# A Fourier transform, a mixture of experts and a gated network in one kernel: a row store moved behind the first gathers, fold tails on VectorE, routing steps placed later

## The chip, the core and the metric

The kernel runs on one core of one Trainium2 chip. The metric is the time of one execution on the device in microseconds. The core's engines work side by side, each through its own list of instructions in order, and wait for one another by semaphores: TensorE (matrix products, with its own queue of weight loads), VectorE (DVE in the profile), ScalarE (ACT), GpSimd (POOL) and SyncE (SP), which here only issues transfers. Sixteen DMA engines carry the transfers that SyncE and GpSimd issue.

## What is computed

The reference transforms the input, sends each row to one of eight experts, and puts the result through a second network:

```python
X = np.fft.fft(np.fft.fft(x, axis=1), axis=2).real        # x: (8, 3072, 256)
x = X.reshape(24576, 256)
logits = x @ w_gate                                       # 8 experts
expert_idx = np.argmax(logits, axis=1); probs = softmax(logits)
# each expert takes the first 768 rows that chose it, in order; other rows give 0
h = np.maximum(np.einsum('ecd,edf->ecf', disp, w1), 0.0)  # (8, 768, 1024)
y = np.einsum('ecf,efd->ecd', h, w2)                      # (8, 768, 256)
out[i] = gate_w[i] * y[expert_idx[i], pos[i]]             # kept rows
h = out @ w_in                                            # (24576, 2048)
return (h / (1 + np.exp(-1.702 * h))) @ w_out
```

At most 6,144 of the 24,576 rows are kept, and since every expert takes the first that choose it, they come from the first rows. The kernel therefore transforms only two and a half of the eight batches, and has a second path behind a condition for inputs where that is not enough.

## The kernel before

A batch (3072 x 256) is a pair of half batches, "units" of 1536 rows; units 0 to 4 are made. For each batch there are two stages on TensorE. In the **S stage** (`fft_s`) the transform along the sequence is a product with cosine and sine tables. A batch's input comes in three parts j, each 1 MB, loaded by SyncE into one of three buffers. Part j is first folded (`fft_fold`): five additions and subtractions on VectorE and a tail of five small instructions (two copies of one column, an addition, a subtraction, a memset), on VectorE for the very first part of the kernel and on GpSimd for all others (line 465). ScalarE then makes `fhi`, a rounded copy, and VectorE the rest `flo`; for j = 2 two small transfers move halves of the part in between. TensorE multiplies in three passes, `fhi` with the table's high and low part (`chi`, `clo`) and `flo` with the high one, and sums into tiles in its accumulation memory, one of eight banks each: `psP0`, `psP2`, `psPE`, `psPO` and the same for Q. The parts are taken in the order 0, 1, 2 in the first batch and 0, 2, 1 in the others. `fft_s_end` combines the tiles on ScalarE and VectorE to `hiP` and `hiQ`. The **row stage** (`fft_d`) multiplies these with the table of the second axis, twelve row tiles t, each a tile `pd` of 128 rows for either half batch, and ScalarE copies them to `xtok`; the logits come out with them.

**Routing** of a unit (`choose`, `count`, `route`) finds each row's expert, its place among the expert's rows and its weight: a chain of some 25 small instructions on VectorE with the counting products `pp` of `oh` on TensorE in the middle. It ends with a store of the unit's rows from `xtok` to the buffer `rows` in device memory, 1.56 MB (or half of it), issued by GpSimd, and with `hold`, which queues the unit for `hold_tables` (tables `lt` and `ls`; VectorE makes both, GpSimd multiplies `lt`) and `hold_sum` (the product `pl`, which turns them into a list of row numbers per expert, `held`). `slots` makes the index list `heldi` from it, and with that GpSimd's indirect transfers gather the rows of a block, three tiles of 128 rows.

The **expert part** takes blocks of 384 rows, 16 in all: `ffn1` for the expert's two layers, `ffn2` for the second network. The first three blocks are those of experts 0 to 2 from units 0 to 2; their gathers are issued in the last row stage, while unit 3's rows and unit 4's are still being routed and stored. For a block VectorE scales the gathered tiles (`xr`, line 878), TensorE transposes them (`pt`, line 898), ScalarE and VectorE split the result to `xhi` and `xlo`. Weights come in pieces of 256 KB, which ScalarE and VectorE split to a high and a low part (`w1h`, `w1l`, `w2h`, `w2l`; lines 355 and 356). SyncE also writes zeros to the output (`zero_out`), 96 stores of 256 KB, two at every second step f of the blocks 0 to 6, the rest later.

The order of an engine's instructions is made by a scheduler from the order in the program, the dependencies and the free buffers and banks; `after` adds an edge that holds for the order alone. So a routing step's place in the program (the hooks `counts` in the S stage and `mid` in the row stage) sets its place on every engine. `CHOOSE` and `ROUTE` are the row tiles of batch 1 at which the first half of unit 2 is chosen and routed. Unit 0 is routed in the middle of batch 1's first part, unit 1 right behind that part, the two halves of unit 2 at row tile 10 of batch 1 and in the first part of batch 2, unit 3 at row tile 2 of batch 2, unit 4 in the first block.

Of the kernel before, what the change touches and what calls it, by code (L numbers as in the profile page):

```python
# [32 lines left out]
ROW = 260  # L33
# [13 lines left out]
LAG = 6  # L47
D1 = 3

J0, J1 = (0, 1, 2), (0, 2, 1)  # L50
# [1 line left out]

FOLD = ((0, "s", 6), (0, 8, 11))
SPLIT = (1,)
CHOOSE, ROUTE = 6, 10
EARLY = 11
LATE, HELD = 3, 7
IN0, IN1 = 5, 7
# [113 lines left out]
class K:  # L172
# [15 lines left out]
    def setup(self):  # L188
        nc, tc = self.nc, self.tc
        enter = self.ctx.enter_context  # L190
        self.c0 = c0 = enter(tc.tile_pool(name="c0", bufs=1))
        self.xr = enter(tc.tile_pool(name="xr", bufs=XR))
        self.ps = enter(tc.tile_pool(name="ps", bufs=8, space=PSUM))
        self.dram = enter(tc.tile_pool(name="dr", bufs=1, space=DRAM))
        n = P + 5 * HT * E // 2 + 3 * HT
        self.smt = c0.tile([P, n], F32, name="smt")
        self.tri = c0.tile([P, 5, P], F16, name="tri")
        self.ident = self.smt[:, 0:P]
        o = P
        self.wt = self.smt[:, o : o + HT * E].rearrange("p (t e) -> p t e", e=E)  # L200
        o += HT * E
        self.seg = {HT: self.smt[:, o : o + HT * E], HT // 2: self.smt[:, o + HT * E : o + 3 * HT * E // 2]}
        self.place = self.smt[:, n - 3 * HT : n - 2 * HT]
        self.tok = self.smt[:, n - 2 * HT : n].rearrange("p (h t) -> p h t", h=2)
        self.base = c0.tile([P, E], F32, name="base")
        self.flag = c0.tile([P, 1], F32, name="flag")
        nc.vector.memset(self.flag, 1.0)
        self.nop = c0.tile([1, 1], F32, name="nop")
        self.sig = c0.tile([1, 1], F32, name="sig")
        nc.vector.memset(self.sig, 0.0)  # L210
        self.disp = self.dram.tile([self.nslot, ROW], F32, name="disp")

        self.rows = self.dram.tile([1 + self.nu * S // 2, ROW], F32, name="rows")
        nst = E * self.capt
        self.held = c0.tile([P, nst], F32, name="held")
        self.heldi = [c0.tile([P, nst], I32, name=f"heldi{i}") for i in range(2)]
        self.idx = None
        self.todo, self.made = [], []
        zt = c0.tile([P, ROW], F32, name="zt")
        nc.gpsimd.memset(zt, 0.0)  # L220
        nc.gpsimd.memset(zt.bitcast(I32)[:, 257:258], OOB)
        self.zt = zt
        nc.gpsimd.dma_start(out=self.rows[0:1, :], in_=zt[0:1])
# [286 lines left out]
    def fft_s(self, b, j, data, hook=lambda i: None):  # L510
        nc = self.nc
        dh, dl = data
        pt, cnt = self.pt, self.cnt
        last = j == JS(b)[-1]
        work = [(half, c, terms) for half in "PQ" for c, terms in self.terms(half, j)]
        if last and j != 2:
            work.sort(key=lambda v: v[1] in (0, 2))
        elif last:
            work.sort(key=lambda v: v[0] == "Q" and v[1] in (0, 2))
        for i, (half, c, terms) in enumerate(work):  # L520
            hook(i)
            n = KC if c == 0 else KC - 2
            at_ = (half, c)
            if at_ not in pt:
                pt[at_] = self.ps.tile([P, KC], F32, name=f"ps{half}{c}", tag="ps")
                cnt[at_] = 0
            row = half == "Q" and c in (0, 2)
            tot = 3 * NJ + row
            ops = [(u[:, g, i, :], w[j][:, t, :n]) for (g, i), t in terms
                   for (u, w) in ((dh, self.chi), (dh, self.clo), (dl, self.chi))]  # L530
            if row and last:
                ops.append((self.sel, self.trs[:, c // 2, :n]))
            for lhsT, rhs in ops:
                nc.tensor.matmul(pt[at_][:, :n], lhsT=lhsT, rhs=rhs, start=(cnt[at_] == 0),
                                 stop=(cnt[at_] == tot - 1))
                cnt[at_] += 1
# [93 lines left out]
    def route(self, xt, mir, u=None, t0=0, chosen=None):  # L630
# [4 lines left out]
        nc = self.nc  # L635
        V = nc.vector
        rp = self.rp
        n = xt.shape[1]
# [34 lines left out]
        V.tensor_copy(out=xt[:, :, 257:258].bitcast(I32)[:, :, 0], in_=tok)  # L673
        if u is not None:
            v = self.rows[1 + u * HT * P : 1 + (u + 1) * HT * P].rearrange("(p i) w -> p i w", i=HT)
            nc.gpsimd.dma_start(out=v[:, t0 : t0 + n], in_=xt[:, :, 0:ROW])
            self.hold(u, t0, n, sloti, pos)
        if u is None or u < self.nu // 2 * 2:
            V.tensor_scalar(out=tok, in0=tok, scalar1=float(S), scalar2=None, op0=ALU.add)
# [319 lines left out]
def kernel(ctx, tc, cap, x, xed, xeb, xt, cm, dc, dct, tri, sel, sm, wg, w1, w2, wi, wo, out):  # L999
# [32 lines left out]
    def fold(b, j):  # L1032
        if b < nb:
            while (b, j) not in xq:
                xload()
            data[j] = k.fft_fold(xq.pop((b, j)), j, (b, j) == (0, J0[0]))

    loads = iter([(b, j) for b in range(1, nb) for j in J1])

# [15 lines left out]
    def route_next():  # L1055
        b, mir, xt, t0, chosen = units.pop(0)
        u = 2 * b + mir
        k.route(xt, mir, u, t0, chosen)
        if u == ua and t0 + xt.shape[1] == HT:
            k.check_full(min(na, cap))  # L1060
# [6 lines left out]
    for b in range(nb):  # L1067
        k.fft_s_begin(b)
        for i, j in enumerate(JS(b)):
            if b == 0 and i == 2:  # L1070
                k.fft_dtables()

            def counts(n, i=i):
                if (i, n) == (0, 4) and units:
                    route_next()
                if b == 0 and (i, n) == (2, 5):
                    k.fft_rows()
                if (b, i, n) == (2, 1, 3):
                    k.hold_tables(2)

            k.fft_s(b, j, data.pop(j), counts)
            while i == 0 and units and b == 1:
                route_next()
            if (b, i) == (1, 0):
                k.hold_tables(2)
            if i == 0 and b:
                folds(b - 1, "n")
        if b == 0:
# [15 lines left out]
        def mid(t):  # L1104
            if b == 1 and t == 0:
                k.hold_sum(2)
                k.hold_tables(2)
            if b == 1 and t == 9:
                k.hold_sum(2)
            if b == 2 and t == 0:  # L1110
                with tc.high_priority():
                    k.hold_sum(2)
                    k.slots(ua)
                xrs[0] = k.ffn_gather(*work[0])
            if b == 2 and t == 2:
                route_next()
                k.hold_tables(2, k.last_gather)
                for n in range(1, AHEAD):
                    xrs[n] = k.ffn_gather(*work[n])
            if t == EARLY and b + 1 == nb and xrs:  # L1120
                xins[0] = k.ffn_in(xrs[0], work[0][2], k.los[2])
            folds(b, t)
            if b in SPLIT and t == CHOOSE:
                xt = xs[0][:, : HT // 2]
                units.append((b, 0, xt, 0, k.choose(xt)))
            if b in SPLIT and t == ROUTE:
                route_next()

        xs = [next(k.slot) for _ in range(1 + (2 * b + 1 < nu))]
        k.fft_d(PQ, xs, mid)  # L1130
# [69 lines left out]
    for n, (e, i0, ns) in enumerate(work):  # L1200
        last = n + 1 == len(work)

        def hook(f, n=n, last=last):
# [22 lines left out]
            if n:  # L1226
                for _ in range(PACE[f]):
                    w64step()
            if f % 2 == 0 and n <= LAG:
                zstep(ZC // 3)  # L1230

        def hook2(f, n=n):
# [96 lines left out]
```

## Time and profile before

| | before |
|---|---|
| three timed runs, median (lowest to highest) | 985.06 us (983.24 to 985.53) |
| the profiled execution, its span | 980.04 us, 978.4 us |
| TensorE, VectorE, ScalarE, GpSimd busy | 925.4, 609.1, 509.7, 225.9 us |
| granted clock of TensorE, mean | 0.98 |
| TensorE idle ahead of its first product | 13.2 us |
| HBM read, written | 51.02, 39.47 MB |

The span runs from the first to the last instruction that the profiler saw. "Busy" adds up an engine's instructions. A list of waits says which engine's instruction ended an idle time. The granted clock is the share of full speed, 2.4 GHz, that TensorE was given; 0.50 is its other level, 1.2 GHz.

### The profile page before, as it was taken

The page shows a single profiled execution, that of the slowest core. Times are in us where ns is not written, and L with a number is a line of the kernel's source. Part 1 is how long each engine was busy: PE and PEld are TensorE (multiplying, and loading weights), DVE is VectorE, ACT ScalarE, POOL GpSimd, SP SyncE. Part 2 cuts the span into 40 slices and gives each one's busy share as a digit, 9 for nine tenths or more (in the row PEclk, how much of TensorE's full clock was granted, in tenths as well). Part 3 has the DMA queues.
Part 4 walks back from the last instruction along what each step waited for, and adds up shares of the span by engine and source line. Part 5 has one row for each costly group of instructions (what it writes and reads, how often), then busy time and mean ns, then how long its engine had stood idle before and what let it go on. Part 6 is the DMA issues. An engine that isn't in the chain of part 4 may idle for free. (4 is left out here: it accounts for less than half of the span.)

```text
span 978.4 us, 15881 instructions
## 1 busy us (share of the span) xinstructions
PE 925.4 (95%) x5950; PEld 904.2 (92%) x5950; DVE 609.1 (62%) x1178; ACT 509.7 (52%) x1056; POOL 225.9 (23%) x259
## 2 busy tenths in 40 slices
PE   3898979999899999999999999999999999999995
PEld 3686769999789999999999999999999999999995
DVE  6688789988994556454645464756535555555552
ACT  4555546656654555354644464646444554555452
POOL 6534525667751011111111100001010110011011
PEclk9899979999899999999999999999999999999998
DMA  8263898978810026001700030301000000000000
GB/s 321 96 189 120 231 290 267 318 246 274 263 45 17 17 87 206 17 18 46 246 17 18 12 92 2 102 1 60 1 17 1 17 17 1 18 17 17 1 17 20
DMA packets 65614, 92.03 MB, mean 94 GB/s; under 512 B 5886, under 2 KB 54262, under 8 KB 64374
## 3 DMA queue, kind: packets, MB, share of 16 engines
q1 hardware_dynamic: 58870, 70.23, 21.9%
q0 software_dynamic: 6656, 20.68, 7.0%
q8 instruction: 49, 0.80, 0.3%
q14 instruction: 39, 0.32, 0.1%
HBM read 51.02 MB, written 39.47 MB: 92 GB/s over the span
## 5 line engine op out<-in xcount | busy, mean ns | idle before, releaser
L975 DVE TENSOR_TENSOR sg<-ph,sg 128x384 f32<-128x384 f32 x256 | 142.7, 557 | 118.0 <-ACT sg L974 117.6
L979 DVE TENSOR_TENSOR gl<-sg,gh 128x384 fp32r<-128x384 f32 x256 | 147.3, 575 | 108.1 <-ACT gh L978 105.7
L978 ACT CAST gh<-sg 128x384 fp32r<-128x384 f32 x256 | 131.1, 512 | 121.1 <-DVE sg L975 121.1
L974 ACT ACTIVATE sg<-ph 128x384 f32<-128x384 f32 x256 | 125.8, 492 | 110.1 <-PE ph L970 105.8
L992 POOL DMA_INDIRECT out<-orow,ix x48 | 47.6, 992 | 558.3 <-ACT orow L991 548.5
L931 DVE SCALAR_TENSOR_TENSOR hl<-ph,hh 128x384 fp32r<-128x384 f32 x128 | 70.9, 554 | 78.8 <-ACT hh L930 78.4
L930 ACT ACTIVATE hh<-ph 128x384 fp32r<-128x384 f32 x128 | 62.8, 493 | 78.9 <-PE ph L925 78.1
L925 PE MATMUL ph<-xhi,w1h 128*128 128x384 f32 x256 | 87.0, 340 | 0.4 <-ACT xhi L355 0.4
L916 PE MATMUL py<-hh,w2h 128*128 128x384 f32 x256 | 87.0, 340 | 0.0
L925 PE MATMUL ph<-xhi,w1l 128*128 128x384 f32 x256 | 86.7, 339 | 0.0
L916 PE MATMUL py<-hl,w2h 128*128 128x384 f32 x256 | 86.0, 336 | 0.6 <-DVE hl L931 0.6
L925 PE MATMUL ph<-xlo,w1h 128*128 128x384 f32 x256 | 86.5, 339 | 0.0
L916 PE MATMUL py<-hh,w2l 128*128 128x384 f32 x256 | 85.6, 334 | 0.0
L864 POOL DMA_INDIRECT xr<-rows,heldi x48 | 52.4, 1092 | 71.2 <-PE pt L898 54.2
L925 PEld LDWEIGHTS ph<-xhi,w1h 128*128 128x128 f32 x256 | 48.9, 191 | 0.8 <-ACT xhi L355 0.8
L916 PEld LDWEIGHTS py<-hl,w2h 128*128 128x128 f32 x256 | 48.0, 188 | 1.3 <-DVE hl L931 1.2
L925 PEld LDWEIGHTS ph<-xlo,w1h 128*128 128x128 f32 x256 | 48.9, 191 | 0.3
L925 PEld LDWEIGHTS ph<-xhi,w1l 128*128 128x128 f32 x256 | 48.9, 191 | 0.0
L916 PEld LDWEIGHTS py<-hh,w2l 128*128 128x128 f32 x256 | 48.1, 188 | 0.0
L916 PEld LDWEIGHTS py<-hh,w2h 128*128 128x128 f32 x256 | 48.1, 188 | 0.0
L356 DVE TENSOR_TENSOR w2l<-wraw,w2h 128x512 fp32r<-128x512 f32 x44 | 36.5, 835 | 16.2 <-ACT w2h L355 15.5
L355 ACT CAST w2h<-wraw 128x512 fp32r<-128x512 f32 x44 | 27.5, 624 | 10.5 <-PE py L916 9.5
(365 smaller groups left out, 2736.3 us busy)
## 6 DMA issues: line engine op xcount, KB each, us to landing
out<-zt SPq DMA_DIRECT2D x96, 256.0 KB, 4.5
wraw<-in_w SPq DMA_DIRECT2D x88, 256.0 KB, 3.4
x<-in_x SPq DMA_DIRECT2D x9, 1024.0 KB, 6.2
rows<-xtok POOLq DMA_DIRECT2D x3, 1560.0 KB, 10.2
wraw<-in_wi SPq DMA_DIRECT2D x8, 512.0 KB, 5.3
wraw<-in_wo SPq DMA_DIRECT2D x8, 512.0 KB, 4.1
cr<-in_cm SPq DMA_DIRECT2D x6, 388.0 KB, 8.2
rows<-xtok POOLq DMA_DIRECT2D x2, 780.0 KB, 7.0
```

What stands on the lines that cost most here:

```text
L355: h = nc.scalar.copy(out=hi, in_=src)
L356: return h, nc.vector.tensor_tensor(out=lo, in0=src, in1=hi.bitcast(F32), op=ALU.subtract)
L864: self.last_gather = nc.gpsimd.indirect_dma_start(out=xr[:, i, :], out_offset=None, in_=self.rows[0 : self.nrow], in_offset=bass.IndirectO ...
L916: nc.tensor.matmul(py[a][:, :n], lhsT=w2[f // 2][v][:, f % 2, a * P : (a + 1) * P], rhs=(hh, hl)[u][:, :n], start=(f == 0 and k == 0), sto ...
L925: nc.tensor.matmul(ph[:, :n], lhsT=w1[f // 2][v][:, a, (f % 2) * P : (f % 2 + 1) * P], rhs=(xh, xl)[u][:, a, :n], start=(k == 0), stop=(k ...
L930: self.last_a = nc.scalar.activation(out=hh[:, :n], in_=ph[:, :n], func=AF.Relu)
L931: self.last_v = nc.vector.scalar_tensor_tensor(out=hl[:, :n], in0=ph[:, :n], scalar=0.0, in1=hh[:, :n].bitcast(F32), op0=ALU.max, op1=ALU. ...
L974: nc.scalar.activation(out=sg[:, :n], in_=ph[:, :n], func=AF.Sigmoid, scale=1.702)
L975: nc.vector.tensor_tensor(out=sg[:, :n], in0=ph[:, :n], in1=sg[:, :n], op=ALU.mult)
L978: nc.scalar.copy(out=gh[:, :n], in_=sg[:, :n])
L979: nc.vector.tensor_tensor(out=gl[:, :n], in0=sg[:, :n], in1=gh[:, :n].bitcast(F32), op=ALU.subtract)
L992: ins = nc.gpsimd.indirect_dma_start(out=out, out_offset=bass.IndirectOffsetOnAxis(ap=xr[:, i : i + 1], axis=0), in_=orow, in_offset=None, ...
```

## The change

It has four parts. The tail of the fold runs on VectorE for all three parts of batch 0, not for the first alone. In `route` the store of a unit's rows is ordered behind the last gather issued so far; there is one when unit 3 is routed, the third tile of block 0. The routing steps stand elsewhere: unit 0 behind the first part of batch 1's S stage, unit 1 three tiles into its second part, the two halves of unit 2 in the first part of batch 2 and behind it; `ROUTE` goes. The second part of these S stages takes its O tiles last, so that two `pp` can have a bank each. And the first block issues no zero stores; the eight follow later.

```diff
-CHOOSE, ROUTE = 6, 10
+CHOOSE = 6
...
+        self.last_gather = None
...
             work.sort(key=lambda v: v[0] == "Q" and v[1] in (0, 2))
+        elif j == 2:
+            work.sort(key=lambda v: v[1] == "O")
...
-            nc.gpsimd.dma_start(out=v[:, t0 : t0 + n], in_=xt[:, :, 0:ROW])
+            ins = nc.gpsimd.dma_start(out=v[:, t0 : t0 + n], in_=xt[:, :, 0:ROW])
+            self.after(ins, self.last_gather)
...
-            data[j] = k.fft_fold(xq.pop((b, j)), j, (b, j) == (0, J0[0]))
+            data[j] = k.fft_fold(xq.pop((b, j)), j, b == 0)
...
             def counts(n, i=i):
-                if (i, n) == (0, 4) and units:
+                if (b and (i, n) == (1, 0)) or (b, i, n) == (2, 0, 3):
                     route_next()
+                if (b, i, n) == (1, 1, 2):
+                    route_next()
+                    k.hold_tables(2)
                 if b == 0 and (i, n) == (2, 5):
                     k.fft_rows()
-                if (b, i, n) == (2, 1, 3):
+                if (b, i, n) == (2, 1, 4):
                     k.hold_tables(2)
 
             k.fft_s(b, j, data.pop(j), counts)
-            while i == 0 and units and b == 1:
-                route_next()
-            if (b, i) == (1, 0):
-                k.hold_tables(2)
...
-            if b in SPLIT and t == ROUTE:
-                route_next()
...
-            if f % 2 == 0 and n <= LAG:
+            if f % 2 == 0 and 0 < n <= LAG:
                 zstep(ZC // 3)
```

Line numbers of the changed program are 1 to 4 higher. The first place is VectorE in the first half batch; `x` are the parts being folded. Before, between the two `flo` of parts 0 and 1 (the last rows of it):

```order
L462 TENSOR_TENSOR x<-x 128x512
L463 TENSOR_TENSOR x<-x 128x512
L457 TENSOR_TENSOR x<-x 128x512
L458 TENSOR_TENSOR x<-x 128x512
L462 TENSOR_TENSOR x<-x 128x512
L463 TENSOR_TENSOR x<-x 128x512
L356 TENSOR_TENSOR flo<-x,fhi 128x1024
```

After, the same stretch from the second row on:

```order
L464 TENSOR_TENSOR x<-x 128x512
L458 TENSOR_TENSOR x<-x 128x512
L468 COPY x<-x 128x1
L469 COPY x<-x 128x1
L470 TENSOR_TENSOR x<-x 128x256
L471 TENSOR_TENSOR x<-x 128x256
L459 TENSOR_TENSOR x<-x 128x512
L472 MEMSET x 128x2
L463 TENSOR_TENSOR x<-x 128x512
L464 TENSOR_TENSOR x<-x 128x512
```

The tail of part 1 stands among the folds of part 2, and the tail of part 2 (the same five rows) follows this and comes ahead of `flo` of part 1.

The second place is VectorE at the end of batch 1's S stage. Before, the four last instructions that make `hiP` and `hiQ`, and what follows them:

```order
L551 TENSOR_TENSOR hiQ<-eb,psQO 128x384
L557 SCALAR_TENSOR_TENSOR hiQ<-psQO,ngs,t_720 128x384
L458 TENSOR_TENSOR x<-x 128x512
L455 TENSOR_TENSOR x<-x 128x1024
L462 TENSOR_TENSOR x<-x 128x512
L463 TENSOR_TENSOR x<-x 128x512
L731 TENSOR_TENSOR held<-held,pl 128x48
```

After, first a piece further ahead in unit 0's routing, then `hiQ`:

```order
L617 TENSOR_TENSOR oh<-eq,q 128x12x8
L459 TENSOR_TENSOR x<-x 128x512
L657 TENSOR_TENSOR pp<-pp,base 128x8
L652 TENSOR_SCALAR q<-q 128x12
L463 TENSOR_TENSOR x<-x 128x512
L357 TENSOR_TENSOR flo<-x,fhi 128x1024
L658 SCALAR_TENSOR_TENSOR inc<-smt,pp 128x96
L464 TENSOR_TENSOR x<-x 128x512
L659 TENSOR_TENSOR sel<-pp,inc 128x8x12
L671 COPY base<-inc 128x8
L456 TENSOR_TENSOR x<-x 128x1024
```

```order
L554 TENSOR_TENSOR hiQ<-eb,psQO 128x384
L698 SCALAR_TENSOR_TENSOR sf<-ti,pos 128x12
L699 CAST tf<-ti 128x12
L560 SCALAR_TENSOR_TENSOR hiQ<-psQO,ngs,t_720 128x384
L735 TENSOR_TENSOR held<-held,pl 128x48
```

The four folds of batch 2's parts that stood behind `hiQ` stand ahead of it among the routing, and one more (line 458) follows between these two pieces.

The third place is GpSimd's queue and VectorE in the last row stage. GpSimd before, from unit 2's second store on (`xr` are the gathers, `xtokx` is unit 3's buffer):

```order
L676 DMA rows_75<-xtok_92 128x6x260
L711 TENSOR_TENSOR lt_1015<-lt_1015,smt_66 128x288
L711 TENSOR_TENSOR lt_1020<-lt_1020,smt_66 128x288
L676 DMA rows_75<-xtokx_93 1536x1x260
L864 DMA xr_1172<-rows_75,heldi0_77 128x260 x3
L864 DMA xr_1246<-rows_75,heldi0_77 128x260 x3
L864 DMA xr_1256<-rows_75,heldi0_77 128x260 x3
```

After:

```order
L679 DMA rows_75<-xtok_92 128x6x260 x2
L715 TENSOR_TENSOR lt_1018<-lt_1018,smt_66 128x288
L715 TENSOR_TENSOR lt_1023<-lt_1023,smt_66 128x288
L868 DMA xr_1172<-rows_75,heldi0_77 128x260 x3
L679 DMA rows_75<-xtokx_93 1536x1x260
L868 DMA xr_1246<-rows_75,heldi0_77 128x260 x3
L868 DMA xr_1256<-rows_75,heldi0_77 128x260 x2
```

VectorE before, from the second gathered tile's scaling on, twelve rows ahead of the third tile's:

```order
L878 TENSOR_SCALAR xr<-xr 128x256
L693 TENSOR_SCALAR ti<-sloti 128x12
L694 SCALAR_TENSOR_TENSOR sf<-ti,pos 128x12
L695 CAST tf<-ti 128x12
L356 TENSOR_TENSOR w1l<-wraw,w1h 128x512
L356 TENSOR_TENSOR w2l<-wraw,w2h 128x512
L710 TENSOR_TENSOR lt<-tf,tri 128x288
L356 TENSOR_TENSOR w1l<-wraw,w1h 128x512
L356 TENSOR_TENSOR w2l<-wraw,w2h 128x512
L713 TENSOR_TENSOR ls<-sf,tri 128x768
L710 TENSOR_TENSOR lt<-tf,tri 128x288
L713 TENSOR_TENSOR ls<-sf,tri 128x768
```

After, from the second tile's scaling on:

```order
L882 TENSOR_SCALAR xr<-xr 128x256
L662 TENSOR_TENSOR sel<-sel,oh 128x96
L669 TENSOR_TENSOR base<-inc,pp 128x8
L663 TENSOR_REDUCE pos<-sel 128x12
L882 TENSOR_SCALAR xr<-xr 128x256
L665 TENSOR_TENSOR over<-pos,q 128x12
L887 TENSOR_SCALAR ix<-xr 128x3
L667 SCALAR_TENSOR_TENSOR sloti<-over,pos 128x12
L697 TENSOR_SCALAR ti<-sloti 128x12
L357 TENSOR_TENSOR w1l<-wraw,w1h 128x512
L357 TENSOR_TENSOR w2l<-wraw,w2h 128x512
```

Unit 3's store went behind the third gather, and the third tile's scaling from behind the four weight splits to ahead of them; the two `lt` and two `ls` still come ahead of `xlo`.

## Rows read from the trace of the kernel before

**Rows 1.** TensorE's waits over the whole span: total us, times, longest us.

```profile
PE psP L534 <- ACT fhi L355: 19.5, 3, 13.2
PE pp L623 <- DVE oh L614: 2.4, 1, 2.4
PE pp L623 <- DVE ex L647: 2.1, 1, 2.1
PE pp L623 <- DVE smt L679: 1.1, 1, 1.1
```

**Rows 2.** Stretches: busy us and instructions by engine, granted clock, DMA share, GB/s.

```profile
core 0: us, PE busy (x) PEld busy (x) DVE busy (x) ACT busy (x) POOL busy (x), PEclk, DMA share, GB/s
23.50:29.40 5.90, 5.49 (x16) 4.98 (x17) 5.70 (x6) 5.00 (x9) 5.90 (x10) 0.50 0.04 14
29.70:31.10 1.40, 1.40 (x9) 1.15 (x7) 0.00 (x0) 0.66 (x2) 1.32 (x7) 1.00 0.00 0
75.32:91.17 15.85, 13.46 (x80) 9.99 (x79) 13.05 (x27) 9.81 (x28) 8.30 (x12) 1.00 0.28 80
91.17:108.06 16.89, 15.81 (x78) 14.57 (x76) 16.86 (x68) 7.36 (x14) 4.96 (x9) 0.90 0.65 189
128.60:135.40 6.80, 6.35 (x20) 5.95 (x21) 4.50 (x18) 2.53 (x6) 1.05 (x1) 0.50 0.71 254
400.00:978.00 578.00, 567.05 (x3867) 566.63 (x3865) 304.17 (x569) 288.42 (x601) 50.76 (x51) 0.99 0.10 33
```

**Rows 3.** Time order, 10 to 36 us: start us, us, engine, line, operation, idle before.

```profile
10.98 0.15 DVE L467 COPY x<-x 128x1 f32<-128x1 f32 x1
...
12.03 1.05 ACT L355 CAST fhi<-x 128x1024 fp32r<-128x1024 f32 x1 [2.51 <-DVE x L471]
...
18.42 1.19 POOL L467 COPY x<-x 128x1 f32<-128x1 f32 x1 [4.02 <-DVE x L463]
...
22.48 1.04 ACT L355 CAST fhi<-x 128x1024 fp32r<-128x1024 f32 x1 [3.92 <-POOL x L471]
...
23.43 1.58 ACT L315 ACTIVATE chi<-cr 128x772 fp32r<-128x772 f16 x2
...
23.57 0.69 PE L534 MATMUL psP<-chi,fhi 128*128 128x386 f32 x1 [3.12 <-ACT fhi L355]
...
27.40 1.11 ACT L315 ACTIVATE clo<-cr,alt 128x384 fp32r<-128x384 f16 x2
...
33.27 1.04 ACT L355 CAST fhi<-x 128x1024 fp32r<-128x1024 f32 x1 [2.01 <-DMA x<-x]
...
34.36 0.44 PE L534 MATMUL psP<-chi,fhi 128*128 128x386 f32 x1 [3.20 <-ACT fhi L355]
```

**Rows 4.** Time order, VectorE from 58 to 76 us.

```profile
58.49 1.23 DVE L455 TENSOR_TENSOR x<-x 128x1024 f32<-128x1024 f32 x1 [3.69 <-DMA x<-in_x]
...
70.02 0.63 DVE L662 TENSOR_TENSOR over<-pos,q 128x12 f32<-128x12 f32 x1
...
74.65 0.90 DVE L557 SCALAR_TENSOR_TENSOR hiQ<-psQO,ngs,t 128x384 f32<-128x384 f32 x1
...
75.99 1.21 DVE L455 TENSOR_TENSOR x<-x 128x1024 f32<-128x1024 f32 x1
```

**Rows 5.** Time order, 108 to 132 us; last the gathers' us from issue to landing.

```profile
108.98 0.99 POOL L676 DMA_DIRECT2D rows<-xtokx  x1 [3.19 <-DVE xtokx L672]
110.34 1.14 POOL L864 DMA_INDIRECT xr<-rows,heldi  x1 [0.38 <-DVE heldi L737]
...
124.52 0.62 ACT L355 CAST w2h<-wraw 128x512 fp32r<-128x512 f32 x1 [0.78 <-DMA wraw<-in_w]
...
127.89 0.76 DVE L878 TENSOR_SCALAR xr<-xr 128x256 f32<-128x256 f32 x1
...
128.70 0.69 PE L898 MATMUL pt<-smt,xr 128*128 128x128 f32 x2 [7.78 <-DVE xr L878]
...
131.19 0.52 PE L925 MATMUL ph<-xlo,w1h 128*128 128x384 f32 x1
...
DMA to landing us min/median/max: 4.4/6.4/8.6
```

## What the change should do, worked out

> **What bounds the kernel now.** TensorE is busy for 95% of the span. The list of what it waited for, read first, shows where the rest is: at `fhi` in the transform, at the counting products `pp`, and at one transpose [rows 1, 5], all ahead of 137 us. In the long second part it has hardly a gap and the DMA engines are a tenth busy [rows 2], so a microsecond gained ahead of it comes out of the total, unless a later wait takes it back. I therefore went gap by gap through the time order of each engine from 0 to 137 us [rows 3 to 5], with the granted clock of the stretches beside it [rows 2]. The times are those of the profiled run, 980.04 us in all (span 978.4). The three timed runs have a median of 985.06, 5.0 above it; I form the sum on the profiled run and carry it over to the median.
>
> A gap costs more than its length. From 23.5 to 29.4 and from 128.6 to 135.4 us, after TensorE had been idle for 3.12 and 7.78 us, the granted clock is 0.50, the 1.2 GHz level, and products start 0.32 us apart; from 29.7 to 31.1, at 2.4 GHz, 0.17 to 0.18 us apart [rows 2]. Such a stretch loses half of its busy time.
>
> **1. The first half batch (0 to 44 us).** TensorE waits 3.12 us at 23.57 and 3.20 us at 34.36, both for ScalarE's `fhi` [rows 3]. The first `fhi` stands behind GpSimd's tail of the fold, from 18.42 to just ahead of 22.48 us, the second behind the same tail and a copy by DMA. The change puts these two tails, five instructions each, on VectorE. What that costs there is seen at the first fold, which has always done it: from the tail's first copy at 10.98 to ScalarE's start at 12.03 it is 1.05 us. VectorE ends the fold just ahead of 18.42, does one fold instruction of 0.6 us, then the tail: it ends at about 19.9, and `fhi` starts 2.6 us earlier than at 22.48. TensorE (busy until 20.45) goes on at 21.1, does four products and then needs `flo`, which now stands behind the second tail: two fold instructions (1.2 us), the tail (1.0) and `flo` (1.5) end at about 23.9. Twenty products more at 0.18 us end at 27.5. ScalarE meanwhile has eight conversions of the third table, from 23.43 to 28.5 in the old run, now right behind the first `fhi`: 20.9 to 26.0 us; two copies of 0.4 us and the third `fhi` follow, and TensorE starts on it at 27.9, not 34.36: 6.5 us earlier. If the clock falls again as it did, the twenty products take 6.4 us, end at 30.3, and the gain is 4.0. I take **-6.0 us** (-6.5 to -4.0), near the first end, because the gap is shorter. The loads that follow are issued when a fold gives its buffer back, so they move along; GpSimd's prelude, which stood behind the tails, only comes earlier.
>
> **2. Routing later, O tiles last (57 to 110 us).** Three gaps at `pp` end here, 2.1, 2.4 and 1.1 us [rows 1]; with the slow stretch behind the two long ones (1.6 us each, half of 3.4) that is 8.8 us. In the new order `pp` stands nine products later in the second batch (1.6 us), and for the split half batch a whole stage later. But the next to be late is VectorE. From 58.49, where it waited 3.69 us for a load of x, it has hardly a pause until `hiQ` ends at 75.55, and TensorE's row stage starts on that at 75.3 to 75.8 [rows 4]. The new order puts five fold instructions ahead of `hiQ` that stood behind it: one like that at 75.99 (1.1 us) and four of half its width (0.6 each), 3.5 us; some 0.7 us of waiting for `pp` comes off. So `hiQ` ends near 78.4. TensorE, done at about 73, stands for 5 us and does the start of its row stage at the lower clock: 2.8 us for `hiQ` and 2 to 3 for the clock. The stage (15.85 us from 75.32) loses its 2.4 us gap, so it ends 2.5 us later than 91.17. The third batch, 16.9 us of which 15.8 are busy and some 3 of these slow [rows 2], has neither gap nor slow stretch and takes 14.2: TensorE is level again. VectorE, which carries the 2.5 us on and saves about 1 of it, ends the third batch's `hiQ` 1 to 1.5 us later, and the first gather starts 1 us later, counted without part 1. I take **+1.0 us**. Bounds: -4, if VectorE keeps up and the gaps just go; +4, if it loses as much again to GpSimd as the 0.63 us at 70.02 for 12 elements shows (0.15 for a copy as small at 10.98) [rows 3, 4].
>
> Here the Trainium skill has a rule: "SBUF — State Buffer", section "SBUF: two separate sides", says that VectorE with two inputs from SBUF and a GpSimd instruction take one shared port pair as an exclusive lock, and the later one stands still. The row at 70.02, which ran beside a GpSimd product, agrees in kind; by this rule the new order, with GpSimd's products in a row, would lose more there, as in rival C.
>
> **3. The first gathers (108 to 137 us).** TensorE waits 7.78 us at 128.70 for the scaling of the third gathered tile, which VectorE does at 127.89 [rows 5]. That is not the gather alone: this scaling stands behind four weight splits, and these behind ScalarE's conversion at 124.52, which waited for its load. These loads were in flight with the store of the fourth half batch, 1.56 MB, issued at 108.98, 1.4 us ahead of the first gather. Gathers take 4.4 us to land at best and 8.6 at worst [rows 5]. The change issues the store behind three gathers, takes the zero stores out of this stretch, and the order that results scales the third tile ahead of the four splits. Count from the first gather, 110.34 in the old run. The third is issued 2.8 us later and lands 6 us after that (between 4.4 and 8.6; the store is gone at first, 1 MB of weights is not): 8.8. Then VectorE scales (0.7 with its neighbours), does four splits (0.6 each), two `lt` and two `ls` (2.5 together) and the first `xlo` (0.5): 14.9. The products that can run without `xlo` are done by then. In the old run the first product with `xlo` starts at 131.19, 20.85 behind the first gather. That is 5.9 us; TensorE now stands twice for 2 to 3 us instead of once for 7.8, and of the 2 us that the lower clock cost after 131.19 I credit 0.6. **-6.5 us**; -10 if the gathers land in 4.4 us and the clock stays up, -2.5 if the weights land as late as before and hold up the splits.
>
> Here the skill has a rule that speaks against the change: "DMA: Bandwidth & Descriptors", section "Queues, rings and completion order", says that a DMA engine takes the queues that have work in turn, packet by packet, so that a store which is issued later still takes its share from the weights. By it the total is that of rival B. No row here separates the two; gathers beside the store took up to 8.6 us.
>
> **4. Zero stores.** Eight stores of 256 KB leave the first block and follow in the seventh block and on, where the DMA engines are a tenth busy [rows 2]. TensorE had no wait for a weight in the first block either. **0 us** (-0.5 to +0.5). The store that goes behind the gathers is read by gathers of the fourth block, some 30 us on; that covers it.
>
> **Sum.** -6.0 + 1.0 - 6.5 + 0 = -11.5 us: 968.5 for the profiled run, **973.5 us** for the median. All good ends together give -21 (964), all bad ones -2 (983).
>
> **Rivals.**
> A, VectorE is not late at the row stages: part 2 brings -4 and the total -16.5, 968.5 us. For it: VectorE stood 3.7 us ahead of this stretch. Against: that wait is for a load that moves along.
> B, the entry still waits for weights: the gathers are there, the splits are not. Part 3 brings -2.5, the total -7.5, 977.5 us. For it: the conversion at 124.52 waited for its load. It is also the case in which the store's place doesn't do what the change says.
> C, slower: VectorE, held up by GpSimd's products, ends the second batch's `hiQ` so late that TensorE stands there and starts its row stage at 1.2 GHz. The slow stretch costs up to 3.4 us (6.8 at half speed, the longest in [rows 2]), every microsecond of `hiQ` counts in full, and the gaps that go give back 5. To eat the 12.5 us of parts 1 and 3, `hiQ` must end some 14 us later than 75.55; at 17 us the total is 988. Against: the 17 us from 58.49 to 75.55 would have to take nearly twice their time.
> D, no difference: the bad ends of all parts at once, 982 to 984 us.
>
> **How the numbers follow.** Forecast 0.55, A 0.20, B 0.13, C 0.05, D 0.07. A measurement of this kernel can tell about 0.3%, 3 us, from no change. Faster by more than that are the forecast, A and B: 0.88; within it D: 0.07; slower C: 0.05. The range 965 to 981 leaves out C, D and the far end of A, somewhat under 2 in 10.
>
> **What would show it.** Right: TensorE's waits for the second and third `fhi` are together under 2.5 us; none is left at `pp`; there is a new wait ahead of the second batch's row stage, at a `pe` or `pd`, with a slow stretch behind it; the first three gathers land in 7 us or less, and the wait at the transposes is under 3 us. Wrong in part 1: over 5 us for the third `fhi`. Wrong in part 2: `hiQ` at its old place, or over 5 us late. Wrong in part 3: the first product with `xlo` more than 18 us behind the first gather.

## The result and the profile after

| | before | after |
|---|---|---|
| side by side, median (lowest to highest) | 984.15 us (978.50 to 985.53), 4 runs | 970.86 us (969.38 to 972.65), 4 runs |
| ratio, 95% interval | | 0.9876 [0.9834, 0.9919] |
| after once more, with more runs of before beside it | 980.63 us, 17 runs | 970.37 us, 6 runs |
| ratio, 95% interval | | 0.9894 [0.9864, 0.9924] |
| the profiled execution, its span | 980.04 us, 978.4 us | 972.65 us, 971.0 us |
| TensorE, VectorE, ScalarE, GpSimd busy | 925.4, 609.1, 509.7, 225.9 us | 923.0, 610.0, 509.1, 227.4 us |

The kernel is 10 to 13 us faster: 973.5 us were predicted, 970.9 measured. The profiled pair differs by only 7.4 us, since the profiled execution of before, 980.04 us, lies below three of the four timed beside it, and that of after is the slowest of its four. Two single executions in the experiments below, of 1833 us (u_route) and 1520 us (o_route), are slow runs and stand in no median. The total came out as predicted; its terms did not, as the traces show below. What TensorE waited for after the change, over the whole span (total us, times, longest us), to be read beside [rows 1]:

```profile
PE psP L537 <- ACT fhi L356: 15.5, 2, 13.3
PE ph L929 <- ACT xhi L356: 3.6, 1, 3.6
PE pt L902 <- DVE xr L882: 2.8, 3, 1.8
PE psP L537 <- DVE flo L357: 2.1, 1, 2.1
PE pd L574 <- DVE ti L697: 1.5, 1, 1.5
PE pp L626 <- DVE pp L657: 0.7, 1, 0.7
```

The wait for the third `fhi`, the long ones at `pp` and the 7.8 us at the first block's transposes are gone. New are 2.1 us for `flo`, 1.5 at the first `pd`, 3.6 for ScalarE's `xhi`, and 1.8 at the transposes of the second block.

**The first half batch.** Time order (start us, us, engine, line, operation, idle before), to be read beside [rows 3]:

```profile
19.12 0.14 DVE L468 COPY x<-x 128x1 f32<-128x1 f32 x1
20.66 1.04 ACT L356 CAST fhi<-x 128x1024 fp32r<-128x1024 f32 x1 [1.98 <-DVE x L472]
21.76 0.44 PE L537 MATMUL psP<-chi,fhi 128*128 128x386 f32 x1 [2.16 <-ACT fhi L356]
22.10 0.86 DVE L470 TENSOR_TENSOR x<-x 128x256 f32<-128x256 f32 x1
23.53 1.22 DVE L357 TENSOR_TENSOR flo<-x,fhi 128x1024 fp32r<-128x1024 f32 x1
24.80 1.01 PE L537 MATMUL psP<-chi,flo 128*128 128x386 f32 x2 [2.07 <-DVE flo L357]
27.43 1.05 ACT L356 CAST fhi<-x 128x1024 fp32r<-128x1024 f32 x1
31.20 0.34 PE L537 MATMUL psP<-chi,fhi 128*128 128x386 f32 x1
```

The third `fhi` is ready at 28.5 us, 0.6 later than worked out, but TensorE comes to it only at 31.20: it stood twice for 2.1 us, and then the clock was low. The third part starts 3.2 us earlier than at 34.36, not 6.5.

That is one execution. In another of the same program (a_again below) TensorE stood for 2.07 and 2.06 us in the same two places, and the clock came back sooner (two products, then the stretch from 24 to 31 us, to be read beside the one below):

```profile
24.63 1.01 PE L537 MATMUL psP<-chi,flo 128*128 128x386 f32 x2 [2.06 <-DVE flo L357]
29.58 0.34 PE L537 MATMUL psP<-chi,fhi 128*128 128x386 f32 x1
...
24.00:31.00 7.00, 6.37 (x29) 6.37 (x30) 5.64 (x8) 4.60 (x10) 6.77 (x12) 0.76 0.71 201
```

In the eight traces that have part 1 as in the change (after, a_again, u_store, u_zero, u_route, i_late, i_xr, and i_flo, where one copy has moved) the third part starts between 29.58 and 31.42 us and the product `pw` at the end of the half batch between 32.36 and 34.19; in the four without it (before, u_fold, o_store, o_route) it is 34.30 to 34.43 and 37.25 to 38.63.

**The stages behind it.** Stretches (busy us and instructions by engine, granted clock, DMA share, GB/s), to be read beside [rows 2]: the slow stretch in the first half batch, the row stage of batch 1, the S stage of batch 2, and a stretch at the start of the second block.

```profile
24.00:31.00 7.00, 6.20 (x19) 6.20 (x20) 5.80 (x8) 4.77 (x10) 6.77 (x12) 0.51 0.58 176
72.62:84.99 12.37, 12.23 (x72) 9.58 (x73) 12.37 (x23) 8.04 (x24) 6.13 (x8) 1.00 0.24 85
84.99:100.87 15.88, 14.45 (x80) 13.02 (x79) 14.99 (x69) 9.22 (x19) 6.70 (x11) 1.00 0.63 199
136.53:140.00 3.47, 3.47 (x23) 3.21 (x24) 2.67 (x7) 0.04 (x1) 0.00 (x0) 0.54 1.04 287
```

Batch 1's row stage and batch 2's S stage now run at the full clock; batch 2's S stage takes 15.88 us instead of 16.89, and ends at 100.87 instead of 108.06.

**The entry.** Time order of GpSimd's first gather and unit 3's store, ScalarE's last weight conversion ahead of the first block, and TensorE's entries to the first and second block; to be read beside [rows 5]:

```profile
103.68 1.14 POOL L868 DMA_INDIRECT xr<-rows,heldi  x1 [3.58 <-DVE heldi L741]
108.02 1.09 POOL L679 DMA_DIRECT2D rows<-xtokx  x1
115.98 0.62 ACT L356 CAST w2h<-wraw 128x512 fp32r<-128x512 f32 x1 [3.49 <-DMA wraw<-in_w]
117.33 0.88 ACT L356 CAST xhi<-pt 128x384 fp32r<-128x384 f32 x2
117.88 0.69 PE L929 MATMUL ph<-xhi,w1h 128*128 128x384 f32 x1 [3.64 <-ACT xhi L356]
135.72 1.28 DVE L882 TENSOR_SCALAR xr<-xr 128x256 f32<-128x256 f32 x3
136.53 1.64 PE L902 MATMUL pt<-smt,xr 128*128 128x128 f32 x6 [1.80 <-DVE xr L882]
```

TensorE now stands because ScalarE, whose queue has `xhi` behind the last `w2h`, waits 3.49 us for that weight to land. And at the second block it stands again, for a scaling that VectorE does behind unit 4's tables, and runs the 3.5 us behind that at a granted clock of 0.54.

How far the run is ahead of the profiled run of before, at points in the order of time:

| point | before | after | ahead by |
|---|---|---|---|
| first product `pw`, end of the first half batch | 37.25 | 33.97 | 3.28 |
| first `psP` of batch 2 | 91.17 | 84.99 | 6.18 |
| first `pd` of batch 2 | 108.06 | 100.87 | 7.19 |
| first gather | 110.34 | 103.68 | 6.66 |
| first product with `xlo` | 131.19 | 120.11 | 11.08 |
| transposes of the second block | 146.45 | 136.53 | 9.92 |
| transposes of the fourth block | 183.28 | 175.53 | 7.75 |

From there to the last block the lead stays at 7.8 to 7.9 us. So in this pair part 1 gave 3.3 us, part 2 gave 3.4 at the gather, the entry 4.4, and the second and third block took 3.3 back.

### The profile page after: what moved, and what is told of

Same layout as the page of the kernel before. It is cut to its first block, busy times and chain, and to the rows that moved or that the text cites. A ratio compares the mean times of both kernels' runs of the same rounds, so it can differ in the third digit from the quotient of the medians.

```text
span 971.0 us, 15883 instructions
## 1 busy us (share of the span) xinstructions
PE 923.0 (95%) x5950; PEld 901.3 (93%) x5950; DVE 610.0 (63%) x1188; ACT 509.1 (52%) x1056; POOL 227.4 (23%) x249
## 5 line engine op out<-in xcount | busy, mean ns | idle before, releaser
L356 ACT CAST w2h<-wraw 128x512 fp32r<-128x512 f32 x44 | 27.5, 625 | 12.9 <-PE py L920 8.8
```

Source lines behind the costliest of these rows:

```text
L356: h = nc.scalar.copy(out=hi, in_=src)
```

## The experiments

Two theories stood against each other. The one on record: part 1 is worth 6.0 us, part 2 costs 1.0, and the store's place behind the gathers brings the entry forward by 6.5. The other, from the trace after: part 1 is worth 3.3, part 2 about 4 as in rival A, and the store holds up the weights for which the entry waits, as in rival B. In the table a kernel's median stands with that of the runs of before that were timed beside it.

| kernel | median us | before beside it | difference | ratio [95%] |
|---|---|---|---|---|
| a_again (the changed kernel) | 970.37 | 980.63 | -10.3 | 0.9894 [0.9864, 0.9924] |
| u_fold (part 1 undone) | 973.26 | 980.04 | -6.8 | 0.9934 [0.9911, 0.9957] |
| u_route (part 2 undone) | 974.74 | 980.04 | -5.3 | 0.9923 [0.9894, 0.9951] |
| u_store (the store's edge undone) | 967.43 | 980.04 | -12.6 | 0.9853 [0.9826, 0.9879] |
| u_zero (part 4 undone) | 970.24 | 980.04 | -9.8 | 0.9889 [0.9861, 0.9916] |
| o_store (before, with the store's edge) | 980.11 | 980.63 | -0.5 | 0.9992 [0.9971, 1.0013] |
| o_route (before, with part 2) | 974.25 | 979.48 | -5.2 | 0.9939 [0.9917, 0.9962] |
| i_late (store behind nine gathers) | 966.15 | 980.63 | -14.5 | 0.9859 [0.9828, 0.9890] |
| i_flo (one copy behind `flo`) | 970.55 | 980.63 | -10.1 | 0.9884 [0.9858, 0.9910] |
| i_flo2 (the tail behind `flo`) | 966.09 | 979.48 | -13.4 | 0.9850 [0.9820, 0.9880] |
| i_xr (second block scaled earlier) | 970.06 | 979.48 | -9.4 | 0.9890 [0.9859, 0.9920] |
| best (i_late and i_flo2) | 963.88 | 980.08 | -16.2 | 0.9822 [0.9792, 0.9852] |

The intervals are 2 to 3 us wide to either side, so the difference of two such rows is uncertain by some 4 us (an estimate from these intervals). Only o_store, i_flo and i_late were timed beside the changed kernel itself (a_again); the others are compared with it through the runs of before. Smaller differences are given by their medians, and what they mean rests on the traces.

**Part 1 undone.**

```diff
-            data[j] = k.fft_fold(xq.pop((b, j)), j, b == 0)
+            data[j] = k.fft_fold(xq.pop((b, j)), j, (b, j) == (0, J0[0]))
```

> The changed kernel with its first part undone: the tails of the folds of parts 1 and 2 of batch 0 go back to GpSimd. By the sum on record this part is worth 6.0 us, so the kernel should be 6.0 us slower than the changed one, about 977. By the trace of the changed kernel it is worth about half: the third part's products start there at 31.20 us against 34.36, since TensorE's wait for flo of part 1 (2.07 us) stands close behind one for fhi (2.16) and the granted clock fell all the same; then it is 3.2 us slower, about 974. The trace should show the third fhi waited for again, some 3 us.

It is 3.5 us less ahead of before than the changed kernel. The third part starts at 34.36 us again, behind a wait of 4.33 us for `fhi`. By the medians part 1 is worth about half of what I gave it; the uncertainty does not exclude the whole.

**The store's edge undone, and alone.**

```diff
             ins = nc.gpsimd.dma_start(out=v[:, t0 : t0 + n], in_=xt[:, :, 0:ROW])
-            self.after(ins, self.last_gather)
```

> The changed kernel without the edge that puts the store of unit 3's rows behind the first gathers. By the sum on record (third part, 6.5 us, nearly all of it this edge) it should be 5 to 6.5 us slower, about 976. If the store only shares the DMA engines and VectorE's order does the rest, the first product with xlo comes at most 2 us later and the total is within 2 us of the changed kernel. A third reading, from the trace of the changed kernel, is that the entry of the first block gains some 5 us and the second block's scaling, which waits behind unit 4's tables on VectorE, gives 3.8 back: then 1 to 2 us slower, with the wait at the second block's transposes gone.

By the medians the sign is the other one: without the edge the kernel is 2.3 us further ahead, and the 5 to 6.5 us of loss that the sum asked for are excluded. GpSimd in it:

```profile
97.65 0.99 POOL L679 DMA_DIRECT2D rows<-xtokx  x1 [2.85 <-DVE tf L698]
104.43 1.15 POOL L867 DMA_INDIRECT xr<-rows,heldi  x1 [4.93 <-DVE heldi L740]
```

With the routing as it now stands the store is ready 6.8 us ahead of the first gather, where in the kernel before it came 1.4 us ahead of it [rows 5]. Nothing is left for the edge to cure; it only moves the store from 97.65 to 108.02, among the weights. ScalarE's last `w2h` without the edge:

```profile
114.83 0.62 ACT L356 CAST w2h<-wraw 128x512 fp32r<-128x512 f32 x1 [0.27 <-DMA wraw<-in_w]
```

That is 10.40 us behind the first gather, instead of 12.30. In the kernel before, the edge alone:

> The kernel before with one edge added: the store of unit 3's rows behind the first three gathers. By the sum on record (third part, -6.5) it is 5 to 6.5 us faster than the kernel before. By what undoing the edge showed (the changed kernel without it is some 3 us faster than with it, since the store then shares the DMA engines with the weights that the first block waits for) it gains nothing or is 1 to 3 us slower: the gathers land sooner, the first product with xlo stays some 20 us behind the first gather, as ScalarE's last w2h waits for its weights.

No difference. The scaling of the third tile did go ahead of the weight splits, as I had said, but the last `w2h` came 15.3 us behind the first gather, and the first product with `xlo` 19.3 behind it, against 20.85 before.

**Part 2 undone, and alone.** Undone is the diff of the routing read backwards (with `ROUTE` and without the sorting of the O tiles); alone, the kernel before has it and nothing else.

> The changed kernel with the routing steps and the order of the tiles as before. By the sum on record (second part +1.0) it should be 1.0 us faster, about 970. By the trace of the changed kernel the part is worth a gain like that of rival A: the row stage of batch 2 starts there 7.2 us earlier than before, of which 3.3 are the first part's, so 3.9 us slower, about 975, with the gaps at pp of 1 to 2.4 us and the slow stretches behind them back.

> The kernel before with the second part alone: the routing steps and the O tiles last. By the sum on record +1.0 us, about 981. By rival A -4.0. By what undoing it showed (the changed kernel with the old routing is some 4.9 us slower) -4 to -5, about 976: no gaps at pp, hiQ of the second batch less than 2 us later than by the old order, and the row stage of the third batch some 4 us earlier.

Undone it gives 5.0 us back, alone it brings 5.2: part 2 is the largest part, with the other sign than on record. TensorE's waits with it undone:

```profile
PE ph L927 <- ACT xhi L356: 8.5, 1, 8.5
PE pp L624 <- DVE oh L615: 2.6, 1, 2.6
PE pp L624 <- DVE ex L648: 1.8, 1, 1.8
```

The gaps at `pp` are back. So is the long wait at the entry, although the store stands behind the gathers: ScalarE waits 3.94 and 3.80 us for two weights, the last at 123.00, 17.4 us behind the first gather. Alone, it has the first product with `xlo` 15.7 us behind the first gather, without any edge on the store.

**Part 4 undone.**

```diff
-            if f % 2 == 0 and 0 < n <= LAG:
+            if f % 2 == 0 and n <= LAG:
```

> The changed kernel with the eight zero stores back in the first block. By the sum on record no difference (within 0.5 us). A rival: at the entry the DMA engines are full until 130 us, so 2 MB more there (some 6 us of transfer at the 300 to 400 GB/s shown there) would push weights back, and the first block would show new waits for weights, 2 to 6 us in all.

No difference that this measurement can tell; part 4 is worth nothing, as predicted.

**The store later still.** All nine gathers of the first three blocks stand ahead of the store:

```diff
             if b == 2 and t == 2:
-                route_next()
-                k.hold_tables(2, k.last_gather)
+                third = k.last_gather
                 for n in range(1, AHEAD):
                     xrs[n] = k.ffn_gather(*work[n])
+                route_next()
+                k.hold_tables(2, third)
```

> The changed kernel with the store of unit 3's rows behind all nine gathers of the first three blocks, not behind the first three. If the store takes DMA time from the four weights that the first block waits for (rival B's mechanism), it now does so some 8 us later, behind them: ScalarE's last w2h of the first block, at 115.98 in the changed kernel, comes 2 to 4 us earlier, and the kernel is 2 to 4 us faster, about 968. If the weights are late for another reason, their own issue above all (105.65 to 108.4 us), nothing changes: within 1 us.

By the medians it is 4.2 us further ahead than the changed kernel beside it. ScalarE's last `w2h` in it, and the store:

```profile
112.65 0.62 ACT L356 CAST w2h<-wraw 128x512 fp32r<-128x512 f32 x1 [1.28 <-DMA wraw<-in_w]
114.03 1.08 POOL L679 DMA_DIRECT2D rows<-xtokx  x1
```

10.9 us behind the first gather (101.77), nearly as without the edge. With all traces side by side: the four kernels whose store leaves well ahead of the gathers or behind all nine (o_route, u_store, i_late, best) have this last `w2h` 10.0 to 10.9 us behind the first gather; of the nine that have it behind the third gather, eight have it 12.3 to 17.4 us behind, and only u_zero, for a reason its trace does not give, at 10.3; the kernel before, whose store leaves 1.4 us ahead of the gathers, has it at 14.2. So the weights give way to a store that is in flight with them. From the issue of the four weights to that conversion it is 10.3 us in the changed kernel, 8.0 in u_store and 8.4 in i_late. In the changed kernel the transfers' queues (packets, MB, share of 16 engines) from 114 to 116 us, when the last of the four weights landed, then from 115 to 118, and from 118 to 121, are:

```profile
q0 software_dynamic: 158, 0.66, 95.1%
q1 hardware_dynamic: 61, 0.10, 12.7%
...
q0 software_dynamic: 159, 0.66, 101.9%
q1 hardware_dynamic: 29, 0.05, 4.4%
...
q0 software_dynamic: 148, 0.52, 96.1%
q1 hardware_dynamic: 44, 0.05, 7.0%
```

q0 is GpSimd's (store and gathers), q1 SyncE's (weights). From 112 to 114 us q1 still had 68%. A weight of 512 KB issued at 108.45 us was still on its way (14.2 us to landing) and others of 256 KB followed from 114.4 us on; from 115 to 121 us 0.10 MB of them all moved.

**The tail behind `flo`.** The wait for `flo` (2.07 us at 24.80) comes from VectorE's order: the second tail stands ahead of it. A first kernel had the edge on the tail's first copy alone:

> The changed kernel with one edge on VectorE: the tail of part 2 of the first half batch stands behind flo of part 1. If the second wait (2.07 us for flo) is what keeps TensorE's clock low from 24.80 us on, flo is there 1.5 us earlier, that wait shrinks to about 0.5, the products behind it run at 2.4 GHz and end near 27.0 us, and the third part waits 1 to 2 us for fhi (near 28.5): its products start 2 to 3 us earlier than at 31.20, and the kernel is 2 to 3 us faster than the changed one, about 968. If the first wait (2.16 us) alone brings the slow stretch, the gain is 0.5 to 1.5 us, as the wait is shorter by 1.5 us and the rest stays.

Only that copy moved, `flo` stayed at 23.55 us, and so did the time. With the edge on all five:

```diff
+        tail = [
...
+            W.memset(x[:, 9:13:2, 0:1], 0.0)]
+        if first and j == J0[2]:
+            for ins in tail:
+                self.after(ins, self.last_flo)
```

> The changed kernel with edges on VectorE that put all five instructions of part 2's tail behind flo of part 1 (in i_flo only the first copy went there: the rest stayed ahead, flo stood at 23.55 us as before and the wait was the same). Now flo can start near 21.9 us and end near 23.1, so TensorE's second wait shrinks from 2.1 to about 0.5 us. If that second wait keeps the clock low, the twenty products behind it end near 26.7 and the third part starts near 28.6 us, as its fhi is ready (31.20 in the changed kernel): 2.6 us earlier, some 968 in all; a wait of 1.8 us for that fhi is then new. If the first wait alone lowers the clock, the products end near 29.6 and the gain is 1.6 us.

By the medians it is 3.1 us further ahead than the changed kernel. TensorE, and its granted clock in two stretches:

```profile
21.93 0.44 PE L541 MATMUL psP<-chi,fhi 128*128 128x386 f32 x1 [2.25 <-ACT fhi L356]
23.30 0.44 PE L541 MATMUL psP<-chi,flo 128*128 128x386 f32 x1 [0.57 <-DVE x L469]
28.71 0.44 PE L541 MATMUL psP<-chi,fhi 128*128 128x386 f32 x1
...
24.40:27.20 2.80, 2.80 (x10) 2.80 (x9) 2.72 (x5) 2.79 (x6) 2.75 (x5) 0.50 0.56 125
27.50:31.00 3.50, 3.50 (x20) 3.20 (x19) 2.54 (x4) 1.85 (x5) 3.33 (x7) 0.99 0.71 272
```

Neither expectation was quite right: the clock fell even with the second wait at 0.57 us, and the third part starts at 28.71, 2.5 us earlier than in the first trace of the changed kernel. But it is only 0.9 earlier than in a_again, whose slow stretch was about as short with the second wait still at 2.06 us. So what the second wait costs stays open.

**The second block scaled earlier.**

```diff
-            if f == IN0 and not last:
+            if f == (IN0 if n else LATE) and not last:
```

> The changed kernel with the scaling of the second block's tiles two steps earlier in the first block, ahead of unit 4's routing and tables on VectorE. If the 1.8 us that TensorE waits there in the changed kernel, with the slow stretch behind it, come from VectorE's order, the wait goes and the kernel is 1.5 to 3.8 us faster, about 968. If the tiles themselves arrive late, VectorE then stands for them earlier, and unit 4's chain behind them moves later: no gain, within 1 us.

The scaling went from 135.72 to 126.88 us, behind no wait, and the transposes lost theirs:

```profile
126.88 0.87 DVE L882 TENSOR_SCALAR xr<-xr 128x256 f32<-128x256 f32 x3
135.52 0.82 PE L902 MATMUL pt<-smt,xr 128*128 128x128 f32 x6
```

So the 1.8 us were VectorE's order, not the gather. The total shows no gain: -9.4 us, against -10.3 for the changed kernel. In that kernel's second trace the wait is 1.2 us at most, so there was less to win than in the first.

**Both together.**

> The changed kernel with two edits together: the store of unit 3's rows behind all nine gathers (i_late, 4.2 us faster than the changed kernel run beside it) and part 2's tail behind flo of part 1 (i_flo2, some 4 us faster). They act in different places, the weights of the first block's entry and the first half batch, so if gains ahead of 137 us simply add, about 962, a ratio to the kernel before of 0.981 to 0.982. If the earlier start only runs into the same weights, whose time is set by when their buffers come free, the two gains overlap: 964 to 966.

963.88 us, 5.9 further ahead than the changed kernel; its interval lies below that of a_again. The two gains, 4.2 and 3.1, add up to 7.3. The median lies near the times expected for an overlap, the ratio, 0.9822, near those expected if the gains add, so this run does not tell the two apart. It is the fastest version here.

## Why the prediction was right, and where it was not

The number was right for the wrong reasons: three of the four terms were off, and the errors nearly cancelled.

**Part 1, -6.0 on record, -3.3 in the trace, -3.5 by undoing it.** The mechanism is the one described, and both `fhi` came 0.6 to 0.8 us later than counted. What failed is the choice within the range: I took the end near the full clock "because the gap is shorter". There were two gaps, 2.16 and 2.07 us, and from 24 to 31 us the granted clock is 0.51. My own count had the second gap (four products from 21.1 us on, then `flo` at 23.9); I did not price it. In this trace even my far bound, 4.0, was passed; in a_again and three others (u_route, i_late, i_xr) the third part starts 4.3 to 4.8 us earlier than before, inside the range, with the clock back sooner. `flo` came at 24.75 and not at 23.9: VectorE has a fold of 0.6 us ahead of the tail's memset, which the order above shows and the count left out (what it counted, 19.9 + 1.2 + 1.0 + 1.5, comes to 23.6), and the second tail's two wide instructions took 0.86 and 0.60 us, where the first tail's took 0.41 and 0.42.

**Part 2, +1.0 on record, -3.4 to -3.9 in the trace, -5.2 and -5.0 by runs.** The gaps went as counted. The step that failed is "TensorE, done at about 73, stands for 5 us". I had the row stage begin with `hiQ`. The stage as it ran:

```profile
69.98 0.63 PE L574 MATMUL pe<-dr,hiP 128*1 128x280 f32 x2
70.45 0.63 PE L574 MATMUL pe<-dr,hiQ 128*1 128x280 f32 x2
72.62 0.74 PE L574 MATMUL pd<-dr,hiP 128*128 128x280 f32 x2 [1.53 <-DVE ti L697]
73.19 0.46 PE L730 MATMUL pl<-lt,ls 128*128 128x48 f16 x12
73.50 0.72 PE L574 MATMUL pd<-dr,hiP 128*128 128x280 f32 x2
74.36 1.18 PE L574 MATMUL pd<-dr,hiQ 128*128 128x280 f32 x4
```

`hiQ` ends at 74.2, 1.9 us late when counted without part 1 (2.85 on record), so VectorE's side was about right. But TensorE had `pe`, two `pd` of `hiP` and `pl` to do first; it stood 1.53 us, and the clock stayed at 1.00. What [rows 4] had shown as the start "on `hiQ`" was an S stage that ended just then: in the run of before no wait stands there. The price is rival A's, about 4 us, but not by its condition: VectorE was late, and TensorE had other work meanwhile.

**Part 3, -6.5 on record.** The first product with `xlo` came 16.4 us behind the first gather (14.9 on record, "wrong if more than 18"), 4.4 us earlier than before. But that was not the store's doing. The edge alone brings nothing, without it the changed kernel is by the medians 2.3 us faster, and part 2 alone brings 15.7. (The 4.4 us "at best" for a gather belongs to a later one: the first nine took 5.3 to 8.6 us before.) The failed step is to read the store beside the first gather [rows 5] as a matter of queue order: it stood there since unit 3's routing was late on VectorE, and once the routing is cleared earlier, the store leaves 6.8 us ahead of the gathers and is no trouble. What ends last at the entry is the last weight, as in rival B, and the entry follows it from kernel to kernel: last `w2h` and first `xlo` product are 10.4 and 15.6 us behind the first gather in u_store, 10.9 and 15.8 in i_late, 12.3 and 16.4 after, 15.9 and 19.9 in i_flo, 17.4 and 21.4 in u_route. The rule in the Trainium skill that I had set against the change ("DMA: Bandwidth & Descriptors", section "Queues, rings and completion order") is borne out in its direction, since a store that is issued later takes time from the weights. Whether the queues take turns the traces don't tell: from 115 to 121 us the packets are 159 to 29 and 148 to 44, but no row shows whether SyncE's queue had packets ready all that time. I had also not seen the second block: 3.3 us of the lead were lost from there to the fourth, 1.8 of them as a wait that VectorE's order made; the rest I put down to the slow stretch behind it, which no run here separates.

**Part 4, 0 on record:** right, -0.5 at most.

**The sum.** On record -6.0 + 1.0 - 6.5 = -11.5. In the profiled pair it is -3.3 - 3.4 - 4.4 + 3.3 = -7.8, and by medians -10.3 and -13.3. Rivals A and B both came in part, one with more gain and one with less, and with part 1 at about half they come out near the forecast. By undoing, the parts are worth 3.5, 5.0, -2.3 and 0.5 us, 6.7 together; the 3.6 us to the -10.3 stay open, within what the intervals allow or as interplay (u_store and o_route differ by parts 1 and 4 alone, and by 7.4 us). Of what was to be seen, the waits for the second and third `fhi` (2.2 us together) and at `pp` were right; the slow stretch ahead of batch 1's row stage did not come; the third gather landed in time, at about 6 us.

## What to carry to other kernels

Before you cure a transfer that stands in the way, ask why it comes at that moment: here the store was late because of a queue on VectorE, and once that was cleared the edge made for it brought nothing and by the medians cost 2 us, by putting the store among the weights that ended last. When you cost a late operand, list all that the waiting engine can do without it, from the program's order and not from where the engine happened to start. And undo each part alone even where the total agrees with the forecast: here it agreed because a gain of about half the size and two misjudged signs made up for one another. Read a stretch at the lower clock from more than one trace: two of the same program differed here by 1.6 us.

## What the runs showed of the hardware

**The same gap costs very different times.** With two waits of 3.0 to 3.2 us at 23.5 and 34.3 us, the kernel before had one slow stretch, from 23.5 to 29.4 us [rows 2]. o_store, which is the same code there with the same waits (3.02 and 3.17 us), fell again at the second and stayed low although TensorE was busy without a pause:

```profile
33.00:37.00 4.00, 2.70 (x8) 2.70 (x9) 1.34 (x2) 1.38 (x3) 1.13 (x3) 0.50 0.89 284
37.00:48.00 11.00, 11.00 (x43) 7.55 (x43) 4.57 (x6) 4.41 (x9) 0.19 (x1) 0.56 0.24 93
```

Its first row stage starts at 49.50 us, 10.9 behind `pw`, where it is 7.2 in the run of before: 3.7 us lost. The changed kernel's two traces differ in the same way: behind waits of 2.16 and 2.07 us products were slow until 31.0 us in one, behind waits of 2.07 and 2.06 us until 27.6 us in the other. The times of before lie mostly between 977.7 and 981 us, with a second group from 982.9 to 985.6; whether such a stretch makes that difference no run here shows.

**GpSimd's queue can nearly shut out SyncE's.** With a store of 1.56 MB and six gathers in flight from GpSimd, SyncE's weights got 4 to 7% of the DMA engines' time for 6 us, and gathers took up to 12.9 us to land, against 8.6 before [rows 5]. Whether the weights were held back in the DMA engines or ahead of them the traces don't tell.
